# Two small products in one pair of PSUM banks, and a step moved in one slot, in a linear-attention kernel with a SoLU layer behind it

## The chip, the cores and the metric

The kernel runs on one core of a Trainium2 chip. The metric is the device time of one execution in microseconds; 621.12 us is the median of three runs of the kernel before (619.44 to 622.68). The engines are named as in the profile: PE is TensorE's matmuls and PEld its weight loads, DVE is VectorE, ACT is ScalarE, POOL is GpSimd and SP is SyncE, which here only issues transfers.

## The reference

Two parts follow each other. The first is a recurrence with a state matrix of 40 x 40 for each of 4 batches and 8 heads, over 768 steps:

```python
for t in range(S):                      # B, H, S, D = 4, 8, 768, 40
    y[:, :, t] = np.einsum('bhd,bhde->bhe', rt, state)
    Sa = np.einsum('bhde,bhe->bhd', state, at)
    state_decay = state * wt[:, :, None, :] - np.einsum('bhd,bhe->bhde', Sa, bt)
    state = state_decay + np.einsum('bhd,bhe->bhde', vt, kt)
```

The second takes the result as 3072 tokens of 320 numbers:

```python
h = x @ w_in                            # 320 x 1024
e = np.exp(h - h_max)
sm = e / (np.sum(e, axis=-1, keepdims=True) + 1e-09)
solu = h * sm
ln = (solu - mu) / np.sqrt(var + 1e-06) * g_ln
return (ln @ w_out)                     # 1024 x 320
```

Everything is computed in fp32; the weights of the second part come as float64 and are narrowed on the chip.

## The kernel before

The recurrence is cut into chunks of 64 steps. Two batches make a pair, so there are N = 24 chunks (12 along the sequence for each of 2 pairs), and each has 16 (batch, head) units. Inside a chunk the dependence of a step on the steps before it is a triangular system, which is solved by way of inverses of its 32 x 32 blocks; VectorE computes these inverses step by step for two chunks at a time.

The order of the work is written out by hand: every engine executes its instructions in the order of the program, and the program is a loop over slots, `for i in range(-1, N + 3 + LAG)`, that runs a software pipeline. With j = i + 5 and m = i - 1, a slot works on several chunks at once:

- On chunk j it prepares the inputs: `front`, `front_b` (transposes of a and of the scaled b), `norm` (16 x 2 small matmuls into the tile `pnt`, a mask on VectorE into `nt`, and the transfer of `nt` to DRAM, from where the inverse is begun).
- On chunk i + 1 it prepares the solve: `bring` and `flip` (the inverse blocks come into the tile `tu`, and VectorE transposes a part of it), `scores` (two times 32 matmuls into `ps`, and two masks on VectorE, into `psi` and into a part of `lv`), `couple` (32 matmuls into `py`, read by ScalarE into `wy`), `close` (32 matmuls into `pz`, read by ScalarE into `tu`), `carried` and `driven` (into `px`, read by ScalarE into `x`).
- On chunk i it solves and reads: `solved` (two times 32 matmuls into `pu`, which ScalarE reads into `nuT` and `lu`), `stated` (4 transposes of the state into `pst`, which ScalarE copies into `s`), `answered` (32 matmuls into `pl`, masked by VectorE into a part of `lu`), `read` (into `pyo`) and `leave` (the new state, and the tokens for the second part).
- On the chunks m - 1, m - 2 and m - 3 it does the second part: `hidden` (the product `h`), `highest`, `exped`, `weighed`, `spreadof`, `folded` (transposes `plnT`) and `output` (the product `po`, in two halves).

Chunks that do not exist are left out, so `norm`, `front` and the other steps on chunk j end with slot 18, `couple` ends with slot 22 and `answered` with slot 23.

PSUM has 8 banks. Four of them are a pool `ps1` with two buffers of two banks each, from which `banks(name)` takes a tile of 128 x 2 x 512. The buffers take turns in the order in which the program calls `banks`: `pu`, `ps`, `py`, `pnt`, `pl`, `pz`, `pyo`, `px` in a slot with all the steps. The first instruction that writes a new tile waits for the readers of the tile that had the buffer before. The framework draws these waits, and those between instructions that use the same tile. Two further banks are the pool `ps3` with single banks in turn (among others `pst`, `po`, `plnT`), and two hold `h`.

In each of the two banks of its pair, `py` uses columns 0 to 127 and `pl` uses columns 0 to 255. A tile of 16 x 2 small matmuls is issued with weight loads of 64 or 40 rows, so that four of them lie side by side in the array.

The tuple `THIN` names slots in which `stated` and `front` come between `solved` and `scores`; in the other slots they come after `scores`. On TensorE the order of a slot around the change is: `pu`, `ps`, `pst`, `pa`, a part of `h`, `pb`, `pei`, another part of `h`, `pcum`, half of `po`, `py`, `pnt`, `pl`, the other half of `po`, `pz`, `pyo` and `px`.

Of the kernel before, what the change touches and what calls it, by code (L numbers as in the profile page):

```python
# [19 lines left out]
Q = 32  # L20
# [4 lines left out]
LAG = 1  # L25


THIN = (5, 15)
LN_EXP = "natural_log_exp_and_others"


# [20 lines left out]
def kernel(  # L52
# [46 lines left out]
    def c_(name):  # L99
        lo, hi = where[name]  # L100
        return cst[:, lo:hi]
# [37 lines left out]
    def banks(name):  # L139
        return ps1.tile([P, 2, 512], FP32, tag="banks", name=name)  # L140

    def bank(name):
        return ps3.tile([P, 512], FP32, tag="bank", name=name)
# [83 lines left out]
    def mean_part(t, lo, hi, start, stop=True):  # L227
        for c in range(lo, hi):
            nc.tensor.matmul(t[:, 0:DM], lhsT=c_("mean"), rhs=w2[:, c, :], start=start and c == lo, stop=stop and c == hi - 1)

    def mean_of(lo, hi, begun):
        t = bank("pmean")
        nc.tensor.matmul(t[:, 0:DM], lhsT=ident, rhs=begun, start=True, stop=False)
        mean_part(t, lo, hi, False)
        return mean_kept(t)

    def mean_kept(t):
        mean = two.tile([P, DM], FP32, tag="osb", name="mean", bufs=1)
        nc.scalar.copy(out=mean, in_=t[:, 0:DM])
        return mean  # L240
# [7 lines left out]
    def half(p):  # L248
        return slice(C * p, C * p + C)

    def rows(p):
        return slice(C * p, C * p + D)
# [3 lines left out]
    def in_turn(tile_of, some=units):  # L256

        lots = {}
        for u in some:
            lots.setdefault(tile_of(*u), []).append(u)  # L260
        lots = list(lots.values())
        return [lot[n] for n in range(max(map(len, lots))) for lot in lots if n < len(lot)]

    def mm(o, lhsT, rhs, start=True, stop=True):
        nc.tensor.matmul(o, lhsT=lhsT, rhs=rhs, start=start, stop=stop, skip_group_check=True)  # L265
# [13 lines left out]
    st = [dict() for _ in range(N + 16)]  # L279
# [11 lines left out]
    def ok(i):  # L291
        return 0 <= i < N
# [12 lines left out]
    def load_values(i):  # L305
        if not ok(i):
            return
        d = st[i]
        d["lv"] = two.tile([P, H, W2], FP32, tag="lv", name="lv", bufs=3)
        d["raw_r"] = two.tile([P, H, D], FP32, tag="raw_r", name="raw_r")  # L310
        load(d["lv"][:, :, C:], v, i)
        load(d["raw_r"], r, i, nc.gpsimd)
# [41 lines left out]
    def tokens(name, bufs=1):  # L354
        return two.tile([P, 2, 4, C], FP32, tag=name, name=name, bufs=bufs)
# [12 lines left out]
    def front(i):  # L368
        if not ok(i):
            return  # L370
        d = st[i]
        t = turned("a", d["raw_a"])
        aT = d["aT"] = tokens("aT", AHEAD)
        nc.vector.tensor_tensor(out=aT[0:W2], in0=t, in1=d["ex"][0:W2, :, :, 0:C], op=ALU.mult)
# [7 lines left out]
    def masked(dst, t):  # L382
        nc.vector.tensor_tensor(out=dst, in0=t.rearrange("p b (j c) -> p b j c", j=4),  # L383
                                in1=tri.unsqueeze(1).unsqueeze(1).to_broadcast([P, 2, 4, C]), op=ALU.mult)

    def keyed(t, u):
        p, q, g, h = u
        return t[rows(h), p, 2 * q + g]

    def valued(t, u):  # L390
        p, q, g, h = u
        return t[rows(q), p, 2 * g + h]

    def norm(i):
        if not ok(i):
            return
        d = st[i]
        t = banks("pnt")
        for u in in_turn(lambda p, q, g, h: (h, p ^ h)):
            p, q, g, h = u  # L400
            j = 2 * q + g
            mm(t[half(p ^ h), h, j * C:j * C + C], keyed(d["bT"], u), keyed(d["aT"], u))
        nt = d["nt"] = tokens("nt", AHEAD)
        masked(nt, t[:, :, 0:256])
        n, at = divmod(i, GRP)
        if at == 0:
            blocks[n] = dram.tile([2 * GRP * H, C, C], FP32, tag="nt_dram", name="nt_dram")
        queue = nc.sync if i < 4 else nc.gpsimd
        queue.dma_start(out=blocks[n].rearrange("(a h x) s c -> a x s h c", a=GRP, x=2)[at].rearrange("x s h c -> (x s) h c"),  # L409
                          in_=nt.rearrange("p h j c -> p (h j) c"))  # L410
# [37 lines left out]
    def bring(i):  # L448
        if not ok(i):
            return  # L450
        d = st[i]
        d["tu"], d["uh"] = tu_t[i % 2], uh_t[i % 2]
        n, at = divmod(i, GRP)
        src = inverse[n].rearrange("(e a h x) c t -> e a h x c t", e=2, a=GRP, x=2)
        for x in range(2):
            queue = nc.sync if i or not x else nc.scalar
            queue.dma_start(out=d["tu"][C * x:C * x + Q, :, Q:2 * Q], in_=src[0, at, :, x].rearrange("h c t -> c h t"))
        for x in range(2):
            nc.sync.dma_start(out=d["uh"][C * x + Q:C * x + C], in_=src[1, at].rearrange("h x c t -> c (h x) t"))
# [7 lines left out]
    def couple(i):  # L467
        if not ok(i):
            return
        d = st[i]  # L470
        t = banks("py")
        for u in in_turn(lambda p, q, g, h: (p ^ h, p)):
            p, q, g, h = u
            j = 2 * q + g
            x = half(p ^ h)
            mm(t[half(p), h, j * Q:j * Q + Q], d["nt"][x, h, j], d["tu"][x, 4 * h + j, 0:Q])
        nc.scalar.activation(out=wy[:, :, :, 0:Q], in_=t[:, :, 0:4 * Q].rearrange("p h (j c) -> p h j c", j=4),  # L477
                             func=AF.Copy, scale=c_("neg_hi"))
# [104 lines left out]
    def answered(i):  # L583
        if not ok(i):
            return
        d = st[i]
        t = banks("pl")
        for u in in_turn(lambda p, q, g, h: (q, p)):
            p, q, g, h = u
            at = (2 * g + h) * C  # L590
            mm(t[half(p), q, at:at + C], d["nuT"][rows(q), p ^ h ^ q, 2 * h + g], valued(d["rT"], u))
        masked(d["lu"].rearrange("p (q x) c -> p q x c", q=2)[:, :, :, 0:C], t[:, :, 0:256])
# [230 lines left out]
    for i in range(-1, N + 3 + LAG):  # L823
        j, m = i + AHEAD, i - LAG
        pieces = shares.get(i, (0, 5, 4, 4) if i % GRP else (3, 5, 4, 5))
        some_weights = narrowed.get(i, (0, 0, 0))
        if i >= 1:
            bring(i + 1)
        if i >= 0:
            load_values(i + 2)  # L830
        narrow(0, pieces[0])

        solved(i)
        if i in THIN:
            stated(i)
            front(j)
        if i >= 0:
            scores(i + 1)
        if i >= 0:
            load_keys(j + 3, "w")  # L840
        load_keys(j + 2, "bak")

        if i not in THIN:
            stated(i)
            front(j)
        hidden(m - 2, ((0, 1),))
        if i == 3 + LAG:
            centred(mean)
        narrow(some_weights[1], pieces[1])
        front_b(j)  # L850
        if ok(j + 2):
            logged(j + 2)
        if i == 1 + LAG:
            first = ps2.tile([P, DFF], FP32, tag="h", name="mean")
            mean_part(first, 0, 2, True, False)
        decay_turned(j + 1)
        hidden(m - 2, ((1, 1),))
        flip(i + 1)
        highest(m - 2)
        scaled(j + 1)  # L860
        left(i - 1)
        if i == 1 + LAG:
            mean_part(first, 2, 3, False)
            mean = mean_kept(first)
        decay(j + 2)
        output(m - 3, 0)

        some(pieces[2])
        if i == 2 + LAG:
            mean = mean_of(3, 6, mean)  # L870
        couple(i + 1)
        exped(m - 2)
        norm(j)
        answered(i)
        weighed(m - 2)
        spreadof(m - 2)
        if ok(j) and j % GRP == GRP - 1:
            begin_inverse(j // GRP)
        if i == 0:
            turn_g()  # L880
        output(m - 3, 1)

        close(i + 1)
        read(i, True)
        carried(i + 1)
        narrow(some_weights[2], pieces[3], ok(j) and j % GRP == GRP - 1)
        by_value(i + 2)
        if ok(m - 1):
            hidden(m - 1, ((2, 0), (2, 1)))
        fence()  # L890
        read(i, False)
        driven(i + 1)
        leave(i)
        begin_narrow(narrowed.get(i + 1, (0,))[0])
        folded(m - 2)
        hidden(m - 1, ((0, 0),))
        attend_kv(i + 2)
        hidden(m - 1, ((1, 0),))
        attend_r(i + 2)
        if i == 2 + LAG:  # L900
            mean = mean_of(6, NF, mean)
# [30 lines left out]
```

## Time and profile before

| | |
|---|---|
| median of three runs | 621.12 us (619.44, 621.12, 622.68) |
| the profiled execution | 616.23 us |
| span of its instructions | 614.4 us |
| mean granted TensorE clock | 0.939 |
| `py` matmuls, busy | 17.3 us (x768) |
| `pl` matmuls, busy | 17.4 us (x768) |
| `pnt` matmuls, busy | 18.4 us (x768) |
| `wy` on ScalarE, busy | 11.4 us (x24, 473 ns each) |
| `pst` transposes, busy | 14.2 us (x88) |

The span reaches from the first instruction to the last; the profiled execution's own time is 1.8 us longer, for what lies around them. Slots 3 to 18 lie between about 125 and 480 us and take some 21.5 us each; slots 19 to 22 lie between about 480 and 560 us and take some 19 to 20 us each, as nothing is prepared for further chunks; the rest is the end of the second part.

In a line of the timeline the columns are: start and duration in us, engine, line, operation, output and inputs by the names of the program's tiles, shapes, and how many instructions were merged; in brackets the idle time of the engine before it and what ended that.

```profile
PE   4463567889899999999999999999999899999994
PEclk9665776889999999999999999999999999999998
```

These two rows of the page cut the span into 40 slices of 15.4 us. Each digit is the busy share in tenths; PEclk is the granted clock. The clock is low in the first quarter and full behind it.

### The profile page before, as it was taken

The page shows a single profiled execution, that of the slowest core. Times are in us where ns is not written, and L with a number is a line of the kernel's source. Part 1 is how long each engine was busy: PE and PEld are TensorE (multiplying, and loading weights), DVE is VectorE, ACT ScalarE, POOL GpSimd, SP SyncE. Part 2 cuts the span into 40 slices and gives each one's busy share as a digit, 9 for nine tenths or more (in the row PEclk, how much of TensorE's full clock was granted, in tenths as well). Part 3 has the DMA queues.
Part 4 walks back from the last instruction along what each step waited for, and adds up shares of the span by engine and source line. Part 5 has one row for each costly group of instructions (what it writes and reads, how often), then busy time and mean ns, then how long its engine had stood idle before and what let it go on. Part 6 is the DMA issues. An engine that isn't in the chain of part 4 may idle for free.

```text
span 614.4 us, 26656 instructions
## 1 busy us (share of the span) xinstructions
PE 545.8 (89%) x11453; PEld 397.3 (65%) x11453; DVE 448.9 (73%) x1262; ACT 265.4 (43%) x548; POOL 257.2 (42%) x424
## 2 busy tenths in 40 slices
PE   4463567889899999999999999999999899999994
PEld 3342457666676777777777777767777676776652
DVE  4797987989968869868968878688698588443431
ACT  4433454655443544444454445445434343342221
POOL 3462264383462472374365355534723631322200
PEclk9665776889999999999999999999999999999998
DMA  8986877575455464564574574554523612310100
GB/s 164 155 162 130 178 158 126 114 153 93 81 108 100 93 119 93 105 114 97 94 131 89 100 130 89 117 106 84 108 57 61 113 43 47 63 34 26 29 19 21
DMA packets 213901, 59.93 MB, mean 98 GB/s; under 512 B 199120, under 2 KB 208952, under 8 KB 213784
## 3 DMA queue, kind: packets, MB, share of 16 engines
q1 hardware_dynamic: 195512, 33.78, 32.6%
q0 software_dynamic: 11568, 19.78, 14.0%
q10 hardware_dynamic: 6704, 4.67, 2.8%
q8 instruction: 90, 1.47, 1.0%
q14 instruction: 27, 0.22, 0.1%
HBM read 40.10 MB, written 13.37 MB: 87 GB/s over the span
## 4 chain that ended last, share of the span: by engine, by line
PE 72%; DVE 17%; DMA 4%; issue 3%; ACT 3%; SPq 1%; POOL 0%; ACTq 0%; DVEq 0%; POOLq 0%
PE po L731 16%; PE h L265 16%; PE pyo L265 8%; DVE uu L438 5%; DVE prod L436 5%; PE pu L265 4%; PE plnT L720 4%; PE ps L265 4%; PE px L265 3%; PE py L265 2%; PE pl L265 2%; PE pz L265 2%; PE pst L513 2%; PE pr L350 2%; PE pcum L333 1%
## 5 line engine op out<-in xcount | busy, mean ns | idle before, releaser
L265 PE MATMUL h<-w_in,xT 128*128 128x512 f32 (+1 forms) x288 | 123.7, 614 | 0.0
L731 PE MATMUL po<-w,lnT 128*128 128x320 f32 x384 | 112.7, 438 | 0.5 <-ACT lnT L721 0.5
L438 DVE TENSOR_TENSOR uu<-uu,prod 128x30 f32<-128x30 f32 (+4 forms) x360 | 103.5, 288 | 12.4
L436 DVE TENSOR_TENSOR prod<-blk,uu 128x30 f32<-128x30 f32 (+4 forms) x360 | 97.6, 271 | 10.9 <-DMA blk<-nt_dram 1.4
L731 PEld LDWEIGHTS po<-w,lnT 128*128 128x128 f32 x384 | 71.0, 190 | 32.6 <-issue 4.1
L409 POOL DMA_DIRECT2D nt_dram<-nt x20 | 18.8, 938 | 119.3 <-DVE nt L383 98.3
L709 POOL TENSOR_TENSOR rs<-c,mhalf 128x1 f32<-128x1 f32 x24 | 13.5, 562 | 112.6 <-DVE c L708 103.7
L383 DVE TENSOR_TENSOR psi<-ps,cst 128x512 f32<-128x512 f32 x24 | 16.6, 691 | 58.3 <-PE ps L265 58.3
L658 POOL DMA_DIRECT2D xT<-x x96 | 48.8, 513 | 0.3 <-DMA blk<-nt_dram 0.3
L265 PEld LDWEIGHTS h<-w_in,xT 128*128 128x128 f32 (+1 forms) x288 | 37.6, 190 | 9.4 <-issue 8.1
L678 DVE TENSOR_REDUCE nmax<-h 128x1 f32<-128x1024 f32 x24 | 28.6, 1193 | 18.6 <-PE h L265 18.6
L420 POOL DMA_DIRECT2D blk<-nt_dram x46 | 37.0, 809 | 9.8 <-issue 6.6
L265 PE MATMUL pyo<-lv,kb 64*64 64x104 f32 x768 | 37.8, 268 | 2.2
L265 PEld LDWEIGHTS pyo<-lv,kb 64*64 64x64 f32 x768 | 23.7, 141 | 21.1 <-issue 21.1
L265 PE MATMUL pyo<-lu,kb 64*64 64x104 f32 x768 | 37.0, 261 | 0.1
L646 POOL TENSOR_TENSOR st<-tot,ex 104x160 f32<-104x160 f32 x44 | 21.7, 511 | 36.4 <-DVE tot L642 26.2
L477 ACT ACTIVATE wy<-py,cst 128x256 f32<-128x256 f32 x24 | 11.4, 473 | 54.5 <-PE py L265 54.5
L562 ACT COPY x<-px 128x320 f32<-128x320 f32 x24 | 10.2, 425 | 55.5 <-PE px L265 55.3
L288 POOL DMA_DIRECT2D raw_r<-in_r_dram x48 | 33.9, 709 | 0.0
L735 ACT ACTIVATE osb<-po,rs 128x320 f32<-128x320 f32 x24 | 12.7, 527 | 48.5 <-PE po L731 32.9
L686 ACT ACTIVATE e<-h,nmax 128x1024 f32<-128x1024 f32 x24 | 26.6, 1108 | 14.3 <-DVE nmax L678 14.3
L692 DVE TENSOR_TENSOR e<-h,e 128x1024 f32<-128x1024 f32 x24 | 29.2, 1217 | 4.6 <-ACT e L686 4.6
(131 smaller groups left out, 1157.5 us busy)
## 6 DMA issues: line engine op xcount, KB each, us to landing
blk<-nt_dram POOLq DMA_DIRECT2D x46, 128.0 KB, 4.6
nt_dram<-nt POOLq DMA_DIRECT2D x20, 256.0 KB, 3.3
raw_w<-in_w_dram SPq DMA_DIRECT2D x48, 80.0 KB
a<-in_a_dram SPq DMA_DIRECT2D x48, 80.0 KB
raw_r<-in_r_dram POOLq DMA_DIRECT2D x48, 80.0 KB, 4.1
lv<-in_v_dram SPq DMA_DIRECT2D x48, 80.0 KB
out_dram<-osb ACTq DMA_DIRECT2D x24, 160.0 KB
raw_b<-in_b_dram SPq DMA_DIRECT2D x44, 80.0 KB
```

Of the source, the lines that this page charges most:

```text
L265: nc.tensor.matmul(o, lhsT=lhsT, rhs=rhs, start=start, stop=stop, skip_group_check=True)
L288: queue.dma_start(out=x[half(p), :, 0:D], in_=ap[2 * bp + p, :, ci * C:(ci + 1) * C, :].rearrange("h t d -> t h d"))
L420: queue.dma_start(out=nb[home:home + Q], in_=blocks[n][:, Q * e:Q * e + Q, Q * e:Q * e + Q])
L436: nc.vector.tensor_tensor(out=t, in0=nb[:, j:j + 1, j + 1:Q].to_broadcast([P, n_c, m]), in1=u[:, 0:n_c, j:j + 1].to_broadcast([P, n_c, m]) ...
L438: nc.vector.tensor_tensor(out=u[:, 0:n_c, j + 1:Q], in0=u[:, 0:n_c, j + 1:Q], in1=t, op=ALU.subtract)
L646: nc.gpsimd.tensor_tensor(out=to3(old), in0=to3(tot[0:W2]), in1=ex[:, :, 2 * q:2 * q + 2, C:].to_broadcast([W2, 2, 2, D]), op=ALU.mult)
L658: nc.gpsimd.dma_start(out=xT[to:to + Q, 2], in_=x[at + P - 3 * D:at + D, 2])
L678: nc.vector.tensor_reduce(out=nmax, in_=d["h"], axis=AX.X, op=ALU.max, negate=True)
L686: nc.scalar.activation(out=e, in_=d["h"], func=AF.Exp, bias=d["nmax"], accum_out=d["esum"])
L692: nc.vector.tensor_tensor(out=d["e"], in0=d["h"], in1=d["e"], op=ALU.mult)
L720: nc.tensor.transpose(out=t[:, j * P:(j + 1) * P], in_=d["e"][:, f * P:(f + 1) * P], identity=ident)
L731: nc.tensor.matmul(d["out"][:, 0:DM], lhsT=d["lnT"][:, f, :], rhs=w2[:, f, :], start=f == 0, stop=f == NF - 1)
```

## The change

It has three edits.

1. In the loop, `banks("pnt")` is called first (where chunk j exists), then `banks("py")`. The tile of `py` is also handed to `answered(i)`, which uses its columns from 128 on, 128 to 383 of each bank. `banks("pl")` is gone, so a slot takes seven pairs in turn in place of eight.
2. `norm`, `couple` and `answered` take the tiles that they are given.
3. Slot 19 joins `THIN`, so `stated(19)` comes before `scores(20)`. `front` of that slot is for chunk 24, which does not exist.

The order of all other instructions is the same on each engine.

```diff
-THIN = (5, 15)
+THIN = (5, 15, 19)
...
-    def norm(i):
+    def norm(i, t=None):
...
-        t = banks("pnt")
+        if t is None:
+            t = banks("pnt")
...
     def couple(i):
...
-        t = banks("py")
+        t = d["py"]
...
     def answered(i):
...
-        t = banks("pl")
+        t = d["pl"][:, :, 4 * Q:]
...
+
+        pnt = banks("pnt") if ok(j) else None
+        if ok(i) or ok(i + 1):
+            st[i]["pl"] = st[i + 1]["py"] = banks("py")
         couple(i + 1)
         exped(m - 2)
-        norm(j)
+        norm(j, pnt)
         answered(i)
```

## The prediction

> **What bounds the kernel now.** I read the page first: who is busy, then the chain that ended last.
>
> ```profile
> span 614.4 us, 26656 instructions
> PE 545.8 (89%) x11453; PEld 397.3 (65%) x11453; DVE 448.9 (73%) x1262; ACT 265.4 (43%) x548; POOL 257.2 (42%) x424
> PE 72%; DVE 17%; DMA 4%; issue 3%; ACT 3%; SPq 1%; POOL 0%; ACTq 0%; DVEq 0%; POOLq 0%
> ```
>
> TensorE is busy 89% of the span and makes 72% of the chain, so time is won or lost where TensorE stands still. The windows 480 to 559 us (slots 19 to 22 of the loop) show PE busy 76.71 of 79.00 us at a granted clock of 1.00: there too a pause of TensorE is a pause of the kernel. Next I asked for the tiles that the change joins, `py` (the couplings) and `pl` (the answers). In the answer for `pl`, under idle time before its instructions:
>
> ```profile
>   ACT wy L477: 4.0, 17
> ```
>
> So in 17 of the 24 slots the first weight load of `pl` (its loads, on PEld) waits for ScalarE's `wy`, which is the reader of `py`; 0.24 us each time. That is the wait the change can be about. The timeline of slot 11, TensorE and then ScalarE, has its anatomy:
>
> ```profile
> 319.88 0.67 PE L265 MATMUL py<-tu,nt 64*64 64x32 f32 x32
> 320.37 0.67 PE L265 MATMUL pnt<-aT,bT 40*64 40x64 f32 x32
> 321.14 0.69 PE L265 MATMUL pl<-rT,nuT 40*64 40x64 f32 x32
> ...
> 320.62 0.47 ACT L477 ACTIVATE wy<-py,cst 128x256 f32<-128x256 f32 x1 [2.01 <-PE py L265]
> ```
>
> `wy` ends at 321.09 and `pl` starts at 321.14. From `py` to `pl` is 1.26 us, though the 32 `pnt` matmuls between need only 0.49. Slot 20, where nothing is normed any more, in the same two views:
>
> ```profile
> 510.78 0.67 PE L265 MATMUL py<-tu,nt 64*64 64x32 f32 x32 [0.43 <-DVE tu L465]
> 511.24 0.70 PE L265 MATMUL pl<-rT,nuT 40*64 40x64 f32 x32
> ...
> 511.50 0.47 ACT L477 ACTIVATE wy<-py,cst 128x256 f32<-128x256 f32 x1 [4.41 <-PE py L265]
> ```
>
> Here `pl` starts 0.46 us after `py` and is nearly over when `wy` begins. The two differ because the pool of bank pairs has two buffers that take turns. With `pnt` in between, `pl` gets the pair that `py` had and waits for its reader; without `pnt`, `pl` gets the other pair.
>
> **Part 1: one pair of banks for `py` and `pl`.** The question is whether, inside one tile, writing columns 128 to 383 must wait for the reader of columns 0 to 127. Slot 19 answers it for the opposite order, TensorE and then VectorE:
>
> ```profile
> 484.05 0.67 PE L265 MATMUL ps<-aT,kT 40*64 40x64 f32 x32
> 484.55 0.30 PE L265 MATMUL ps<-rT,vT 40*64 40x64 f32 x8
> 486.01 0.58 PE L265 MATMUL ps<-rT,vT 40*64 40x64 f32 x24 [1.16 <-issue]
> ...
> 486.65 0.69 DVE L383 TENSOR_TENSOR psi<-ps,cst 128x512 f32<-128x512 f32 x1 [5.49 <-PE ps L265]
> ```
>
> `psi` reads columns 0 to 255 of `ps`, which the first 32 matmuls had written by 484.72. VectorE sat idle 5.49 us and started only at 486.65, after the last of the second 32 (486.59), which write columns 256 to 511. So this program orders the users of a bank by the bank, not by columns. `nuT` in slot 11 does the same: the first half of `pu` is done at 312.24, ScalarE is idle from 312.23, `nuT` starts at 312.80 after the second half (312.69). I take it that the write of `pl` will likewise be ordered behind the read by `wy`.
>
> [...]
>
> With that, by slots:
>
> *Slots 0 to 18* (19 slots with a `pnt` and a `pl`). `pl` waits for `wy` before and after: 0. `pnt` is now taken ahead of `py`, so the two swap what they wait for. `pnt` waits for the readers of `pu` (`nuT`, `lu`): `py`, ahead of it on TensorE, did that before: 0. `py` waits for the two masks that read `ps`. In slot 11 the second ends at 315.00 and `py` starts at 319.88, and `py` needs in any case VectorE's transpose of `tu` (ends 318.83), which is behind the masks in VectorE's order. In every slot from -1 to 22 that transpose ends after the masks, by 0.35 us (slot 22) to 7 us: that is the cover, and the cost is 0. `pz` still gets the pair of `pnt`, `pyo` that of `pl`, `px` that of `pz`: same readers, 0. Seven pairs a slot in place of eight only swap the two pairs from slot to slot.
>
> *Slots 19 to 22* (no `pnt`, both `py` and `pl`). A new wait: `pl` starts 0.05 us after `wy` ends, the distance in slot 11. From the starts and ends in these slots: slot 19, `wy` ends 492.56, so 492.61 for 491.82, +0.79; slot 20, 511.98, so 512.03 for 511.24, +0.79; slot 21, 531.00, so 531.05 for 530.28, +0.77; slot 22, 549.91, so 549.96 for 549.19, +0.77. Sum **+3.12 us**. Queued behind the waiting `pl` on TensorE are half of `po` (8 matmuls), `pz`, `pyo`, `px`; for these wait the mask of `lu` on VectorE, and on ScalarE `osb` and the copies into `tu` and `x`. Nothing swallows the delay: in slots 19 and 20 `py` waits for VectorE's transpose (0.33 and 0.43 us), but VectorE itself was idle for 1.84 us before the `psi` of slot 20, waiting for `ps`, so it moves along; in 21 and 22 TensorE waits for nobody there. *Slot 23* has no `py`: 0. Were the chain from `lu` to the transpose what sets slots 19 and 20, only 21 and 22 would count, +1.54: the low end.
>
> **Part 2: four transposes `pst` before `ps` in slot 19.** The same four, no DMA and no other queue; ScalarE's order (`nuT`, `lu`, `s`) stays, and its `s` may start sooner. The `front` of that slot is empty (chunk 24 doesn't exist). What is in reach is the 1.16 us hole in `ps` above, for which no engine is named. The trace has a packet of 16,384 bytes of the instruction queue (90 packets, 1.47 MB) from 483.44 to 484.47, so I read it as TensorE out of instructions until 485.95. [...]
>
> If the end of the hole is fixed by the fetch, eight instructions (4 loads, 4 matmuls) more ahead of it put it 4 matmuls earlier, so 28 instead of 24 follow it, at 0.5 us for 32 (484.05 to 484.55): `ps` ends 4 x 0.0156 = 0.06 later. TensorE saves the 0.5 us of `pst` afterwards, but `py` waits in that slot for the transpose (491.22, TensorE free at 491.03), whose chain begins with `ps`. So +0.06. Bounds: if the hole goes altogether, `ps` ends 0.9 earlier, **-0.9** (1.16 less the extra change of shape); if there is no help, the order of slot 15 against slot 16 is the price: `pu`'s second half to `h` takes 2.70 there (398.43 to 401.13) and 2.43 here (420.32 to 422.75), **+0.27**. I take +0.06, as it follows from the rows of that very slot.
>
> **Sum:** 0 + 3.12 + 0.06 = +3.2 on a profiled execution of 616.23 us (span 614.4 and 1.8 around it), 619.4. The median of the three shown is 621.12, 4.9 above the profiled one; on it the forecast is **624.3 us**.
>
> **Rivals.**
> 1. *Columns decide.* If the framework lets `pl` write beside the read, the wait goes where it is now. `pnt` to `pl` is 0.80 in loads (320.34 to 321.14) where `py` to `pnt` is 0.46, so 0.34 in each of 17 slots, -5.8, and nothing new in the tail; at three slots `pz` waits for VectorE's `nt` afterwards (3.8 us in all), which may take some back. 621.1 - 5.8 = **615.3**, faster. For: it is the only wait between the two tiles. Against: `psi` and `nuT` above. It decides from the first slot: the 0.24 us before `pl` would be gone.
> 2. *The wait comes, but slot 19 gains its hole*, or half of the new waits are swallowed by VectorE's chain: +3.1 - 0.9 = +2.2, or +1.6: **622.7 to 623.3**. For: VectorE's work, not TensorE's, is what `py` waits for in 19 and 20. Against: its idle 1.84 us.
> 3. *The wait comes, and instructions fall elsewhere*: a new hole like the one of 1.16 us in another slot, as fewer or more waits shift what stands in a block of instructions: +4.4, **625.5**. Only one such hole of over 1 us is seen in the main slots now, so it is the exception.
>
> **How the numbers follow.** A measurement here tells some 0.5% (3.1 us) from no change: under 618.0 is faster, over 624.2 slower. Forecast 0.64; its own range is 622.5 to 625.8 (run medians spread by 1.6 either way), and it lies astride the bound, 0.36 slower and 0.28 same. Rival 1: 0.11, faster. Rival 2: 0.13, same. Rival 3: 0.12, 0.11 of it slower. Together faster 0.11, same 0.42, slower 0.47. The range goes down to 617.5, which leaves out the first rival's heart, and up to 626.5.
>
> **What would show it.** In the profile after: `pl` waits for `wy` in 21 slots in place of 17, by 0.24 us as before in the early ones and some 0.75 us in slots 19 to 22, where `pl` starts 0.05 after `wy` ends. `py` and `pnt` wait for nothing new. The `ps` of slot 19 has a shorter hole, and its `psi` starts within 0.1 of where it did. Slot 11 keeps its 1.26 from `py` to `pl`. Wrong I'd be if `pl` started before `wy` ended anywhere, or if TensorE's lag in slot 19 was gone at the `ps` of slot 20.

## The result and the profile after

| | before | after |
|---|---|---|
| median, runs side by side | 618.94 us (615.89 to 622.68, 20 runs) | 622.60 us (619.99 to 628.39, 20 runs) |
| ratio | 1 | 1.0070, 95% interval 1.0054 to 1.0086 |
| span of the profiled execution | 614.4 us | 621.7 us |

The ratio is not the quotient of the two medians, which is 1.0059. By the ratio the change makes the kernel slower by 0.70%, some 4.3 us; the medians differ by 3.7 us. Forecast were 3.2 us (624.3 on a median of 621.12), with a range of 617.5 to 626.5. Two further comparisons of the same kernel gave 1.0069 (1.0037 to 1.0100) and 1.0072 (1.0041 to 1.0103). So the sign and the place were right, and the sum is above the forecast, by about a third if the ratio is taken and by 0.5 us if the medians are.

The two profiled executions differ by 7.3 us, which is more than the kernels do. The profile before was a quick one of its kernel (616.23 us against a median of 618.94).

The page of the profile after has the same work, and a chain that ended last which is much like the one before:

```profile
span 621.7 us, 26680 instructions
PE 556.6 (90%) x11453; PEld 404.9 (65%) x11453; DVE 450.3 (72%) x1262; ACT 265.5 (43%) x548; POOL 259.0 (42%) x424
PE 70%; DVE 15%; DMA 5%; ACT 3%; issue 3%; SPq 2%; ACTq 0%; POOL 0%; DVEq 0%; POOLq 0%
```

The answers now stand in the tile `py`, so the answer for that tile shows who waited on whom. From the list of what ended idle time before other instructions:

```profile
who waited for it (us, times):
  ACT wy L478: 55.3, 24
  POOL nt_dram L410: 21.0, 3
  DVE lu L383: 7.6, 4
  PEld py L265: 6.6, 20
  PE py L265: 2.4, 4
```

Weight loads of the answers wait for `wy` 20 times and 6.6 us (before: 17 times, 4.0 us). Sixteen of these are the old wait, 0.24 us each in slots 3 to 18. The other four are new: in slots 19 to 22 the load waits 0.69 to 0.71 us, and there the matmul stands as well, 0.58 to 0.59 us each time (the line with 4 times and 2.4 us). Slot 11, TensorE and then ScalarE:

```profile
323.82 0.67 PE L265 MATMUL py<-tu,nt 64*64 64x32 f32 x32
324.31 0.67 PE L265 MATMUL pnt<-aT,bT 40*64 40x64 f32 x32
325.08 0.69 PE L265 MATMUL py<-rT,nuT 40*64 40x64 f32 x32
...
324.56 0.47 ACT L478 ACTIVATE wy<-py,cst 128x256 f32<-128x256 f32 x1 [2.02 <-PE py L265]
```

The answers (`py<-rT,nuT`) start 1.26 us after the couplings and 0.05 after `wy` ends, just as before. Slot 20:

```profile
515.77 0.67 PE L265 MATMUL py<-tu,nt 64*64 64x32 f32 x32 [0.43 <-DVE tu L466]
517.02 0.69 PE L265 MATMUL py<-rT,nuT 40*64 40x64 f32 x32 [0.58 <-ACT wy L478]
...
516.49 0.47 ACT L478 ACTIVATE wy<-py,cst 128x256 f32<-128x256 f32 x1 [4.41 <-PE py L265]
```

Here 1.25 us lie between them, 0.46 before the change. TensorE stands until the reader of the other columns is done.

Where the 7.3 us arose can be followed by the start of `py` in each slot, after minus before, in these two profiles:

| slot | -1 | 2 | 3 | 10 | 18 | 19 | 20 | 21 | 22 | end |
|---|---|---|---|---|---|---|---|---|---|---|
| after - before, us | +1.37 | +1.79 | +3.80 | +3.93 | +4.43 | +4.20 | +4.99 | +5.66 | +6.46 | +7.26 |

From `py` of slot 19 on every slot adds 0.67 to 0.80, 3.06 in all. The way from `py` of slot 18 to `py` of slot 19 gives back 0.23. The 4.4 us up to slot 18 are there before the change can act (slot -1) or fall in between slots 2 and 3, where the granted clock is still rising and falling; from slot 3 to slot 10 they grow by 0.13. In eleven profiles of this study in which nothing but the change, or a part of it, was altered up to there, `py` of slot 3 starts between 144.07 us (the profile before) and 148.40 us, and the four of the kernel after alone cover 144.68 to 148.40. So most of the 4.4 us is scatter of the start. The step between slots 2 and 3 goes with the clock: the last stretch at a granted clock of 0.50 lasts 3.4 us in the profile before (126.4 to 129.8) and 13.7 us in the one after (123.3 to 136.9). In three of the eleven it lasts 3.4 us, and these agree in that step to 0.01 us; in the other eight it lasts 13.7 us, and the step is 1.83 to 2.07 us longer.

### The profile page after: what moved, and what is told of

It is laid out like the page before. It is cut to its first block, busy times and chain, and to the rows that moved or that the text cites. A ratio compares the mean times of both kernels' runs of the same rounds, so it can differ in the third digit from the quotient of the medians.

```text
span 621.7 us, 26680 instructions
## 1 busy us (share of the span) xinstructions
PE 556.6 (90%) x11453; PEld 404.9 (65%) x11453; DVE 450.3 (72%) x1262; ACT 265.5 (43%) x548; POOL 259.0 (42%) x424
## 4 chain that ended last, share of the span: by engine, by line
PE 70%; DVE 15%; DMA 5%; ACT 3%; issue 3%; SPq 2%; ACTq 0%; POOL 0%; DVEq 0%; POOLq 0%
PE po L732 16%; PE h L265 15%; PE pyo L265 7%; DVE uu L439 5%; PE py L265 4%; PE pu L265 4%; PE plnT L721 3%; DVE prod L437 3%; PE px L265 3%; PE ps L265 3%; PE pz L265 2%; DMA uu_dram<-uu 2%; PE pst L514 2%; PE pr L350 2%; PE pk L350 1%
## 5 line engine op out<-in xcount | busy, mean ns | idle before, releaser
L439 DVE TENSOR_TENSOR uu<-uu,prod 128x30 f32<-128x30 f32 (+4 forms) x360 | 105.9, 294 | 12.4
L437 DVE TENSOR_TENSOR prod<-blk,uu 128x30 f32<-128x30 f32 (+4 forms) x360 | 95.1, 264 | 11.4 <-DMA blk<-nt_dram 1.8
```

Source lines behind the costliest of these rows:

```text
L437: nc.vector.tensor_tensor(out=t, in0=nb[:, j:j + 1, j + 1:Q].to_broadcast([P, n_c, m]), in1=u[:, 0:n_c, j:j + 1].to_broadcast([P, n_c, m]) ...
L439: nc.vector.tensor_tensor(out=u[:, 0:n_c, j + 1:Q], in0=u[:, 0:n_c, j + 1:Q], in1=t, op=ALU.subtract)
```

## The experiments

All ratios are against the kernel before, run on the same chip in the same job.

### The shared pair of banks alone

```diff
-THIN = (5, 15, 19)
+THIN = (5, 15)
```

(against the kernel after)

> The shared pair of banks alone; slot 19 keeps its old order. Theory: the four waits of pl for wy in slots 19 to 22 are the whole loss, 4 x 0.79 = +3.1 us, ratio 1.005, and py to pl is 1.26 us in slot 19 and after, as in the slots before. The hole in the ps of slot 19 (1.16 us) is still there. Rival (the shared pair also costs in the first slots, as the +4.4 us before slot 13 of the one profile after suggests): ratio 1.009 to 1.012, and again some 2 us more from slot 2 to slot 3.

Measured: 1.0046 (1.0022 to 1.0070). From `py` of slot 19 to the end the profile adds 3.01 us, as good as with the whole change, and from slot 1 to slot 4 the distance to the profile before stays at 1.82 us. That the 2 us between slots 2 and 3 are absent here doesn't settle the rival: the two later profiles of this kernel have them (2.07 and 1.93 us), the second profile of the kernel after has not (0.01), and the one with slot 19 in `THIN` alone has them without the shared pair (1.83). They go with the length of the slow stretch of the clock, not with the banks. The four waits are the bulk of the loss. What the theory says of the hole was wrong: the hole in the `ps` of slot 19 was gone although the order there is the old one. More on that below.

### Slot 19 in THIN alone

```diff
-THIN = (5, 15)
+THIN = (5, 15, 19)
```

(against the kernel before)

> The kernel before with slot 19 in THIN alone. Theory: the hole of 1.16 us in the ps of slot 19 goes, the change of shape costs some of it back, -0.2 us to -0.3 us as in the profile after, ratio 0.9995. Prediction as it stands on record: +0.06, with bounds -0.9 and +0.27. Rival (the move is a loss in itself): ratio 1.001 or more and the hole moves to another tile.

Measured: 1.0008 (0.9984 to 1.0032), which tells none of the three apart in time. In the profile the hole was still there:

```profile
486.79 0.28 PE L265 MATMUL ps<-rT,vT 40*64 40x64 f32 x4
488.08 0.68 PE L265 MATMUL ps<-rT,vT 40*64 40x64 f32 x28 [1.01 <-issue]
```

It stands 4 matmuls earlier than in the kernel before, with 28 behind it in place of 24, as the prediction has it. But from `py` of slot 18 to `py` of slot 19 it took 0.60 us longer than in the profile before. The gain of 0.2 to 0.3 us that was expected did not come.

### A pair of its own for the answers in the tail

```diff
-            st[i]["pl"] = st[i + 1]["py"] = banks("py")
+            st[i + 1]["py"] = banks("py")
+            st[i]["pl"] = st[i + 1]["py"] if ok(j) else banks("pl")
```

(against the kernel after)

> The kernel after, but where no pnt stands between (slots 19 to 22) pl has a pair of its own again. Theory: py to pl is back at 0.46 to 0.49 us in these slots, the loss of the change is gone but for its gain in slot 19: -0.2 us against before, ratio 0.9995. Rival (part of the loss lies in the first slots): ratio 1.002 to 1.007, as nothing there is altered.

Measured: 1.0002 (0.9975 to 1.0028). Slot 20 of its timeline:

```profile
514.43 0.67 PE L265 MATMUL py<-tu,nt 64*64 64x32 f32 x32 [0.43 <-DVE tu L466]
514.89 0.70 PE L265 MATMUL pl<-rT,nuT 40*64 40x64 f32 x32
```

The distance is 0.46 us again, and from slot 19 to the end the profile is even with the one before (-0.15 us). All that is left of the change here, the shared pair in 19 slots, the swap of waits between `py` and `pnt`, and the moved step, costs nothing that this comparison can tell (its interval is -1.5 to +1.7 us). The loss lies in four slots.

### The wait laid under another product

```diff
         norm(j, pnt)
+        if not ok(j):
+            output(m - 3, 1)
         answered(i)
...
-        output(m - 3, 1)
+        if ok(j):
+            output(m - 3, 1)
```

(against the kernel after)

> The kernel after, with the second half of po between py and pl on TensorE where there is no pnt (slots 19 to 22; the pair of banks stays shared). Theory: the wait for wy is still drawn but lies under the 2.3 us of po, so no weight load of pl waits there and the tail costs nothing: -0.2 us against before, ratio 0.9995, and 3 us faster than the kernel after. Rival (something else of the shared pair slows the tail): ratio 1.004 to 1.005 as with the banks alone, with the lost time before another tile.

Measured: 1.0035 (1.0012 to 1.0058). The expected 0.9995 is out; the time is near the rival's, and as the rival has it the lost time stands before another tile. The timeline of slot 20 shows which. TensorE, and then the mask on VectorE:

```profile
514.63 0.67 PE L265 MATMUL py<-tu,nt 64*64 64x32 f32 x32 [0.43 <-DVE tu L466]
515.23 2.42 PE L732 MATMUL po<-w,lnT 128*128 128x320 f32 x8
517.58 0.69 PE L265 MATMUL py<-rT,nuT 40*64 40x64 f32 x32
518.09 0.62 PE L265 MATMUL pz<-uh,wy 64*64 64x32 f32 x32
519.15 0.69 PE L265 MATMUL pyo<-rT,s 40*64 40x64 f32 x32 [0.44 <-DVE lu L383]
...
518.41 0.69 DVE L383 TENSOR_TENSOR lu<-py,cst 128x512 f32<-128x512 f32 x1 [0.66 <-PE py L265]
```

The wait for `wy` is gone, as the theory has it. But the answers now start 2.95 us after the couplings (0.46 in the kernel before), so the mask that reads them ends only at 519.10, and `pyo`, which gets this pair of banks next, waits for it. Before, that mask lay under the same half of `po`. Slots 19 to 21 are longer by 0.59, 0.48 and 0.48 us than before, and from `py` of slot 19 to the end it is 2.58 us. The wait was exchanged for another, not hidden.

### The cover taken away in every slot

```diff
-        norm(j, pnt)
         answered(i)
+        norm(j, pnt)
+        normed(j)
+        answers_masked(i)
```

(against the kernel after; `normed` and `answers_masked` hold the two masks, in their old order)

> The kernel after, with pl ahead of pnt on TensorE in every slot; the masks on VectorE keep their order. Theory: pnt no longer covers part of the wait; py to pl stays 1.26 us, but the 0.46 us of pnt now come behind pl and not under the wait: 17 slots x 0.46 = +7.8 us on top of the 2.9 of the change, +10.7 us against before, ratio 1.017. Rival (TensorE has slack in slots 2 to 18 and a pause there is free): ratio 1.005 to 1.007 as the change itself.

Measured: 1.0184 (1.0155 to 1.0213). Slot 11 on TensorE:

```profile
327.32 0.67 PE L265 MATMUL py<-tu,nt 64*64 64x32 f32 x32
328.59 0.69 PE L265 MATMUL py<-rT,nuT 40*64 40x64 f32 x32 [0.59 <-ACT wy L485]
329.10 0.65 PE L265 MATMUL pnt<-aT,bT 40*64 40x64 f32 x32
```

Each slot from 5 to 10 is longer by 0.46 to 0.56 us than in the kernel before, mostly 0.47. Slots 11 to 17 add 0.38 to 0.48 us each, but for one that has a hole of 0.91 us with no engine named and adds 1.57. So a pause of TensorE costs its full length, or nearly so, in these slots as well, and what made the wait cheap there, before and after, is that `pnt` fills 0.46 of its 0.80 us.

### The answers beside the norm

```diff
         couple(i + 1)
         exped(m - 2)
+        if ok(i) or ok(j):
+            t = banks("pnt")
+            if ok(j):
+                st[j]["pnt"] = t
+            if ok(i):
+                st[i]["pl"] = t[:, :, 256:]
         norm(j)
         answered(i)
+        normed(j)
+        answers_masked(i)
```

(against the kernel before; the masks are taken out of `norm` and `answered` as in the experiment above)

> The kernel before with pl in the pair of pnt (columns 256 to 511) in place of that of py, and both sets of matmuls ahead of both masks; old THIN. Theory: no reader stands between pnt and pl, so pl starts 0.46 us after pnt, py to pl falls from 1.26 to 0.95 us in slots 2 to 18: 17 x 0.32 = -5.4 us, ratio 0.991; the mask of nt waits for the matmuls of pl too, which costs nothing as VectorE comes to it 0.9 us after these end in slot 11. Rival (TensorE isn't the bound there, VectorE or the transfers take it back): ratio 0.996 to 1.000 with pz or py waiting longer for VectorE.

Measured: 0.9957 (0.9933 to 0.9981), half of what the theory had. The wait itself is gone everywhere, as slot 11 shows:

```profile
322.28 0.67 PE L265 MATMUL py<-tu,nt 64*64 64x32 f32 x32
322.77 0.67 PE L265 MATMUL pnt<-aT,bT 40*64 40x64 f32 x32
323.26 0.65 PE L265 MATMUL pnt<-rT,nuT 40*64 40x64 f32 x32
...
323.02 0.47 ACT L483 ACTIVATE wy<-py,cst 128x256 f32<-128x256 f32 x1 [2.01 <-PE py L265]
```

Both sets run while `wy` reads the other pair; 0.98 us from `py` to the answers, and 0.33 us less per slot from slot 9 to slot 11. Part of the gain was taken back. In this profile slots 2 and 3 gain only 0.13 and 0.02 us, as `pyo` waits there for ScalarE's copy into `tu` (0.49 and 0.55 us). In the slots behind, holes of TensorE for which no engine is named took back more, the longest within `ps` of slot 9, 1.77 us:

```profile
270.47 0.67 PE L265 MATMUL ps<-aT,kT 40*64 40x64 f32 x30
272.91 0.21 PE L265 MATMUL ps<-aT,kT 40*64 40x64 f32 x1 [1.77 <-issue]
```

### The same with slot 9 in THIN

```diff
-THIN = (5, 15)
+THIN = (5, 9, 15)
```

> The kernel with pl beside pnt in one pair (e4_answers_beside_norm), and slot 9 in THIN, where its profile had a hole of 1.9 us within ps. Theory: the hole goes, as with slots 5 and 15, less 0.3 us for the change of shape: ratio 0.993, 1.6 us under e4. Rival (the hole comes and goes by itself from execution to execution, or moves to another tile): ratio 0.995 to 0.997 as before.

Measured: 0.9946 (0.9926 to 0.9965), between the two, and its interval overlaps that of the kernel without the move. In its profile the hole in slot 9 is down to 0.34 us. By its median it is the fastest kernel of the study, but that slot 9 in `THIN` adds to it is not shown. Nor is that a hole had gone so from slots 5 and 15: these two are in `THIN` in every kernel here, and the expectation took it as given.

### The changed kernel and the banks alone, again

Five runs took the same two kernels once more, unaltered.

> The changed kernel once more beside the others. Theory: +2.8 us from its tail, ratio 1.0045. Rival (there is 1.5 us more in it than the tail shows, as the first comparison of 1.007 says): ratio 1.0065 to 1.008. Either way py to pl of 1.26 us in slots 19 to 22; what differs from the first profile before slot 2 tells how much of the start varies by itself.

Measured: 1.0069. Slot 19 is longer than in the first profile, and the windows on TensorE (start and end, length, busy time, granted clock, DMA share, GB/s) show a fall of the clock behind the new wait:

```profile
494.00:498.90 4.90, 3.66 (x73) 1.00 0.43 71
498.90:502.30 3.40, 3.40 (x13) 0.54 0.02 5
502.30:506.00 3.70, 3.70 (x134) 0.97 0.04 11
```

The same stretch of the first profile, with the clock at 1.00 throughout:

```profile
492.50:497.40 4.90, 3.16 (x72) 1.00 0.42 71
497.40:500.80 3.40, 3.40 (x84) 1.00 0.02 5
500.80:504.50 3.70, 3.61 (x137) 1.00 0.12 32
```

Both middle windows begin with the same half of `po`. In 3.4 us TensorE issued 13 matmuls in the one and 84 in the other; that half of `po` took 4.11 us for 2.42.

> The changed kernel, for its time beside that of the banks alone on one chip, and for one more profile of slot 19. Theory: in slot 19 TensorE stands before py (0.65 to 1.15 us) and again before pl (0.58), and in some executions the granted clock falls to half for 3.4 us there, as in one of two profiles so far, which makes the po behind it 1.7 us longer: ratio 1.006 to 1.007, against the 1.0045 of the tail's waits alone. Rival (the 1.007 was chance): 1.0045.

Measured: 1.0072 (1.0041 to 1.0103), with the clock at 1.00 in slot 19.

> The shared pair of banks alone, without slot 19 in THIN, beside the kernel after. Theory: the same waits before py and pl in slot 19, so the same chance of a fall of the clock: within 0.15% of the kernel after, ratio 1.005 to 1.007. Rival (the move of pst itself is what costs the difference between 1.007 and 1.0046): ratio 1.0045 again and 1.5 us under the kernel after.

Measured: 1.0040 (1.0013 to 1.0067), 623.84 us against 622.25 us of the two medians. The difference between the kernels is 1.6 us, about as the first two ratios have it (0.0024 of 619.7 us, 1.5 us), but the intervals overlap. On the other chip, in two jobs, the medians of the two kernels are 623.44 us (banks alone) and 623.32 us, which is no difference.

> The changed kernel, one profile more. py to pl is 1.25 us in slot 19 and 1.26 in 20 to 22, whatever the clock. If the granted clock falls behind the wait in slot 19, that slot is 1.7 us longer than in the first profile; if not, equal to it within 0.1 us from py on.

The clock stayed at 1.00 in slot 19, and 1.25 and 1.26 us lie between couplings and answers. From `py` of slot 19 to the end it adds 3.01 us (3.06 in the first). So one of four profiles of this kernel shows the fall.

> The shared pair of banks alone, one profile more. The hole of 1.16 us within the ps of slot 19 was there before the change and is gone in the first profile of this kernel although its order there is the old one. If it comes and goes from execution to execution it is found in one of the three profiles of this kernel; if the shared pair moved it for good, in none.

The hole is back:

```profile
489.48 0.29 PE L265 MATMUL ps<-rT,vT 40*64 40x64 f32 x7
490.94 0.58 PE L265 MATMUL ps<-rT,vT 40*64 40x64 f32 x25 [1.17 <-issue]
```

The two other profiles of the very same kernel have none in slot 19. It comes and goes from execution to execution.

## Why the prediction was right, and where it was not

**Who is ordered behind whom.** Right. The prediction read from `psi` and `nuT` that the framework orders the users of a bank by the bank and not by columns. That columns don't count is shown; as `py` and `pl` share one tile here, bank and tile are not told apart. The profile after shows it in the order that counts here: answers behind `wy` in every slot that has both, 0.05 us after its end from slot 3 on and 0.14 before. The first rival (columns decide, 615.3 us) is out. What it hoped for was real, though: where the answers share a pair with `pnt`, whose reader comes later, the wait does go, at 0.9957.

**Slots 0 to 18: 0.** Right; the profile has the same 1.26 us, and the kernel that keeps the shared pair only in these slots is at 1.0002. The named covers held: from slot 5 to slot 18 `py` and `pnt` wait for nothing that they didn't wait for before.

**Slots 19 to 22: +3.12.** Right. The profile after gives 0.79, 0.79, 0.77 and 0.77 more between `py` and the answers, and 3.06 us from `py` of slot 19 to the end; five other profiles with the wait (two of the kernel after, the one with the fall of the clock not counted, and three of the banks alone) give 3.01 to 3.26. Hardly anything swallowed it (0.12 us in slot 20), which rules out the half of the second rival in which VectorE's chain sets these slots. That TensorE has no slack in the other slots either was tested by taking the cover away.

**Slot 19 in `THIN`: +0.06.** The size was harmless, but this step failed. Where the hole stands was right: 28 matmuls of `ps` lie behind it in place of 24. What the prediction took as fixed, that it is there and when it ends, is not. With the old order it is there in the profile before and in one of three of the banks alone. With the new one it is 0, 0.19, 0 and 0.47 us in the four profiles after, and 1.01 in the one with slot 19 in `THIN` alone. The sign that was to show it, `psi` within 0.1 us of its old place, failed too: measured from `py` of slot 18 it starts 0.67 us earlier in the first profile after.

The prediction also overlooked what stands behind the hole. It took the way from `ps` through VectorE to `py` as the one that counts. Where the hole is absent, VectorE is done early and its transpose waits for the transfer of the inverse blocks from DRAM, and `py` waits for the transpose. VectorE, and then TensorE, in slot 19 of the first profile after:

```profile
494.97 0.45 DVE L466 STREAM_TRANSPOSE tu<-tu 128x256 f32<-128x256 f32 x1 [0.39 <-DMA tu<-uu_dram]
...
495.56 0.67 PE L265 MATMUL py<-tu,nt 64*64 64x32 f32 x32 [1.15 <-DVE tu L466]
```

With the banks alone, where the hole is absent, the transpose waits 0.73 and 0.75 us for the same transfer. So a hole that goes altogether brings some 0.6 us there, not the 0.9 of the lower bound. Measured by `py` of slot 18 to `py` of slot 19, against the profile before: old order without the hole -0.60 and -0.58, with it +0.04; new order without it -0.23 in the first profile and -0.64 in the third, with 0.19 of it -0.23, with 0.47 +0.06 and with 1.01 +0.60. The -0.23 and the -0.64 differ by the transfer alone: the transpose can start 20.68 us behind `py` of slot 18 in the one and 20.27 in the other. So no price of the moved step can be read from these rows, and that it keeps the hole away could not be shown.

**The sum: 3.2 forecast, 4.3 measured by the ratio, 3.7 by the medians.** The waits alone account for 3.1 and give 1.0046 and 1.0040 when the shared pair is measured alone (2.5 to 2.9 us). The whole change is at 1.0070, 1.0069 and 1.0072. The moved step is all that differs, but without the waits it shows as 1.0008 and 1.0002 only, and the medians put the two kernels 1.6 us apart on one chip and level on another. The fall of the clock in slot 19 (1.7 us) was seen in one of four profiles of the kernel after and in none of three of the banks alone, which is too few to say that the move brings it. So whether the change costs more than its four waits stays open.

**The third rival** (instructions fall elsewhere, +4.4) comes nearer to the ratio than the forecast does, but its mechanism is not shown. The programs with the shared pair have one instruction more on TensorE and 23 more on VectorE (all of them semaphore instructions: 209 for 208 and 205 for 182 in the profile after), and a hole of 1.43 us within `ps` of slot 9, absent in the profile before, shows in two of four profiles after. But the kernels with the banks alone, with a pair of its own in the tail and with the wait behind `po` have the same program up to slot 19, and none of their five profiles has that hole. It shows in the kernel with the answers beside the norm as well.

## What to carry to other kernels

Two outputs in one PSUM tile were ordered as one here, whatever their columns: the answers stood 0.58 to 0.59 us for the reader of the couplings in each of slots 19 to 22. So before putting two together, look for the reader of the first and ask what TensorE does until that reader is done. Put an output beside one whose reader comes later than its own matmuls, and issue both sets ahead of both readers; that took the wait away here (0.98 us from `py` to the answers in slot 11 for 1.26, ratio 0.9957), where sharing with a tile read at once brought it to four more slots (3.06 us in the profile after). A pause seen in one profile with no engine behind it should be looked for in a second profile of the same kernel before an instruction is moved for its sake.

## What the runs showed of the hardware

**The clock changed in steps of 3.41 us, and a short pause was followed by a slow step twice.** In all fourteen profiles the granted clock is 0.50 or 1.00, and its changes lie whole multiples of 3.41 us apart (in the profile before the stretches between them last 3.41 to 20.48 us, and then one lasts 481.28). In the second profile after it fell for one such step twice in the main slots. One fall, at 273.9 us, comes behind a hole of 1.43 us in slot 9: `pst` took 1.08 us for the usual 0.64, and the slot was 3.3 us longer, more than twice the hole. The other, at 499.1 us, comes behind the two pauses of slot 19 (0.65 us before `py`, 0.58 before the answers). The fourth profile has the same hole in slot 9 and pauses of 0.67 and 0.58 us in slot 19, each time within one step, and the clock stayed at 1.00; slot 9 was 1.7 us longer there. In the steps ahead of the two falls TensorE was busy 1.98 and 2.17 of 3.41 us, in those of the fourth profile 1.97 and 2.15 of 3.40, so busy time alone doesn't decide it, and what does stays open.

**Instruction holes scattered in time, but not in place.** Within dense runs of small matmuls TensorE stood for 0.3 to 1.8 us with no engine named, in different slots in different executions of the same kernel. The traces show where. Between 140 and 570 us the fourteen profiles have 27 holes of over 0.3 us, and all 27 begin 193 or 194 instructions behind a multiple of 256 in TensorE's stream, weight loads counted. A trace has 90 packets of 16,384 bytes on one instruction queue (`q8` of the page) and 23,146 instructions on TensorE, one packet for every 257. Each of the 27 holes ends 1.24 to 1.88 us behind the end of such a packet (the one of 1.16 us in the profile before 1.53 behind it), and over all 1,042 places of this kind the next instruction never comes sooner than 1.19 us behind its packet (median 3.4). That these are late fetches of instructions is the author's reading of place and time; no run altered the fetch itself. The other 1,015 of the 1,042 places have no hole of over 0.3 us.
